# The first batch's start on one Trainium2 core: order of the q and k loads, tails first, and other zero products

## The chip, the core and the metric

The kernel runs on one core of a Trainium2 chip. The metric is the time of one execution on the device in microseconds (us), as the median of several runs; lower is better. A core has a matrix engine (TensorE, "PE" in the profile, its weight loads "PEld"), a vector engine (VectorE, DVE), a scalar engine (ScalarE, ACT), GpSimd (POOL) and a sync engine (SyncE, SP) that mostly issues transfers. Each engine works through its own list of instructions in order. Transfers run on 16 DMA engines; SP's go through one queue, GpSimd's through another.

## The reference, cut to what matters

Eight batches; 8 heads; 576 positions; head width 64; model width 512, hidden width 2048. First a linear attention whose features are scaled rectified values:

```python
def phi(x, c, s):
    r = np.maximum(x, 0.0)
    return np.concatenate([r * c, r * s], axis=-1)     # 64 -> 128 features
q_p, k_p = phi(q, cos_w, sin_w), phi(k, cos_w, sin_w)  # weights depend on the position alone
kv  = np.einsum('bhsf,bhsd->bhfd', k_p, v)
z   = np.sum(k_p, axis=2)
num = np.einsum('bhsf,bhfd->bhsd', q_p, kv)
den = np.einsum('bhsf,bhf->bhs', q_p, z)[..., None] + 1e-06
x   = num / den                                        # heads side by side: 576 x 512
```

Then a mixer: `h = x^T U V` (rank 32, over positions), `u = x + h^T`, and `out = u + relu(u w_ch1) w_ch2`.

## The kernel before

**Tiling.** The 576 positions of a batch are 64 groups of nine. An even partition of a 128-row tile holds a group's first five positions, an odd one its last four. So a batch's q is a tile `qst` of 128 partitions x 8 heads x 5 columns ("chunks") x 64: chunks 0 to 3 are full, chunk 4, the tail, has data in even partitions only. `load_even` fills all five chunks of the even partitions, `load_odd` four of the odd ones; k (`kst`) and v (`vst`) are laid out alike, and for batch 0 the tail chunk is set to zero first (lines 125 to 127), so that its odd rows are zero.

**Order.** The program is written out by hand: each engine's list follows the order of the Python statements (a manual schedule). Waits between engines come from semaphores at the true dependencies. From batch 1 on, a list of slots interleaves work; this case is about what lies ahead of it, batch 0.

**Batch 0.** `q_prep` (L305 on ScalarE, L307 on VectorE) makes one chunk's cosine or sine half from `qst`. `qtr_mm` (L394) transposes a chunk on TensorE, eight heads into one PSUM bank, and `qtr_evac` copies it to `q_pT` (tail: `q_tlT`). `k_prep` makes k's features; `z_mm` (L1219) sums them per head with a matrix of ones, in the order of `KORD`, into the bank `xz`, and `z_sb` is z in bf16. Then `first_chain`: `v0` is v in bf16, cast in four pieces of two heads; `kv0_mm` (L353) makes kv of heads 0 to 3, `den_mm` (L1227) the denominators of all heads, `recip` their reciprocals; `kv_unit(b, 1)` (L341) makes kv of heads 4 to 7; `xh_mm` (L1235) multiplies by kv, and `xh_norm` (L1244, VectorE) or `xh_norm_act` (L1267, ScalarE, chunk 3 of heads 0 to 3) divides. `a_mm` (L465), `open_mm` (L1258) and `uTd_mm` (L565) make u transposed; `g1_open` (L727) and `g1_main` (L710) are w_ch1's products, for which ScalarE makes `hid`. `g2_part` (L781) is w_ch2's product, from slot 16 on.

**Zero products.** `keep_warm` (L202) multiplies zeros by zeros, 512 columns wide or narrower, so that TensorE is busy before the data come; its results are not read.

**Gates.** `G_.tensor_copy(out=mark..., in_=X)` makes GpSimd wait for X before it issues the weight loads behind it (`w1_load`, `w2_load`, four each, one per quarter of the hidden width); a one-element transfer `nc.sync.dma_start(out=mark2, in_=X)` does the same on SP for the loads of batch 1.

Of the kernel before, what the change touches and what calls it, by code (L numbers as in the profile page):

```python
# [17 lines left out]
def kernel(  # L18
# [11 lines left out]
    nc = tc.nc  # L30

    B = 8
    H = 8
    S = 576
    D = 64
    E = D + 1
    P = 128
# [11 lines left out]
    def tail(b):  # L49
# [16 lines left out]
    qst, kst, vst = (  # L66
        pool.tile([P, H, 5, D], FP32, tag=n, bufs=1, name=n) for n in ("qst", "kst", "vst")
    )
# [4 lines left out]
    def load_even(dst, src, b, h0=0, h1=H):  # L73
        nc.sync.dma_start(
            out=dst[0:P:2, h0:h1].rearrange("m h c d -> m h (c d)"),
            in_=nines(src, b)[:, h0:h1, 0 : 5 * D],
        )

    def load_odd(dst, src, b, h0=0, h1=H):
        nc.sync.dma_start(  # L80
            out=dst[1:P:2, h0:h1, 0:4].rearrange("m h c d -> m h (c d)"),
            in_=nines(src, b)[:, h0:h1, 5 * D : 9 * D],
        )
# [19 lines left out]
            out=w1_bf[:, :, cs], in_=moe_w_ch1.rearrange("(d p) n -> p d n", p=P)[:, :, cs]  # L103
        )

    def w2_load(n):
        js = slice(n * 4, n * 4 + 4)
        nc.gpsimd.dma_start(
            out=w2_bf[:, js, :], in_=moe_w_ch2.rearrange("(j p) n -> p j n", p=P)[:, js, :]
        )  # L110

    def cast(eng, o, i):
        if eng is nc.scalar:
            nc.scalar.activation(out=o, in_=i, func=AF.Copy, bias=0.0, scale=1.0)  # L114
        else:
            eng.tensor_copy(out=o, in_=i)  # L116
# [5 lines left out]
    stU = st_uv[:, S : S + 5 * R].rearrange("p (c r) -> p c r", r=R)  # L122

    zero = pool.tile([P, 512], BF16, tag="o_sb", bufs=2, name="zero")
    V_.memset(zero, 0.0)
    for x in (qst, kst, vst):
        V_.memset(x[:, :, 4, :], 0.0)
    load_odd(qst, q, 0)
    load_even(qst, q, 0)
    load_odd(kst, k, 0)  # L130
    load_even(kst, k, 0)
    for h0 in (0, 4):
        load_odd(vst, v, 0, h0, h0 + 4)
        load_even(vst, v, 0, h0, h0 + 4)
# [264 lines left out]
    def qtr_evac(b, c, eng, t):  # L399
        if c < 4:  # L400
            cast(eng, q_pT[b][:, c, :, :], t)
        else:
            cast(eng, q_tlT[:, :, tail(b)], t[:, :, 0:P:2])
# [803 lines left out]


    TL = (0, 1, 2, 3, 4)
    KORD = (0, 1, 2, 4, 3)  # L1210

    z_sb = const.tile([P, H], BF16)

# [3 lines left out]
    def z_mm(b, c, z):  # L1217
        for h in range(H):
            nc.tensor.matmul(  # L1219
                out=z[:, h, :], lhsT=k_p[b][:, c, h, :] if c < 4 else k_tl[:, h, :],  # L1220
                rhs=ones, start=(c == 0 and h == 0), stop=(c == 3 and h == H - 1),
            )

    def den_mm(b, d, cs):
        for c in cs:
            for h in range(H):
                nc.tensor.matmul(  # L1227
                    out=d[:, c, h, :], lhsT=qT_of(b, c, h),
                    rhs=z_sb[:, h : h + 1].to_broadcast([P, 12]), start=True, stop=True,
                )  # L1230
# [32 lines left out]
    def xh_norm_act(b, c, h0, rec, acc):  # L1263
        x_alloc(b)
        rows = slice(0, P) if c < 4 else tail(b)
        for i in range(4):
# [3 lines left out]
                scale=rec[rows, c, h0 + i : h0 + i + 1],  # L1270
            )

    def first_chain(b, xz, z, v_ps):
        def fill(n):
            for _ in range(n):
                nc.tensor.matmul(
                    out=xz[:, 1, P:512], lhsT=zero[:, 0:P], rhs=zero[:, 0:384],
                    start=True, stop=True,
                )

        d = xz[:, 1, 0:480].rearrange("p (c h n) -> p c h n", h=H, n=12)
        rec = pool.tile([P, 5, H], FP32, tag="rec5", bufs=1, name="rec5")
        cast(V_, v0[:, 0:2], vst[:, 0:2])
        cast(V_, z_sb, z[:, :, 0])
        cast(V_, v0[:, 2:4], vst[:, 2:4])
        cast(V_, v0[:, 4:6], vst[:, 4:6])
        qtr_evac(b, 4, A_, t_q[4])
        kv_sb[b] = pool.tile([P, H, E], BF16, tag="kv", bufs=2, name="kv")
        acc = bank([P, 4, D], FP32, *G3, "kv_ps")
        kv0_mm(b, acc, (0, 1))  # L1290
        den_mm(b, d, (0, 1, 2))
        kv0_mm(b, acc, (2, 3))
        cast(A_, V_bf, v_ps.rearrange("r (c p) -> r c p", c=4))
        cast(A_, kv_sb[b][:, 0:4, 0:D], acc)
        cast(A_, v0[:, 6:H], vst[:, 6:H])
        den_mm(b, d, (3, 4))
        recip(rec, d[:, :, :, 0])
        x0 = [xh_mm(b, c, 0, *G3) for c in ORD[0:2]]
        kv_unit(b, 1, *T1, A_)
        x0 += [xh_mm(b, c, 0, *t) for c, t in zip(ORD[2:5], (G3, OA, OB))]  # L1300
        xh_norm_act(b, ORD[4], 0, rec, x0[4])
        for n in range(4):
            xh_norm(b, ORD[n], 0, rec, x0[n])
        x1 = [xh_mm(b, c, 4, *t) for c, t in zip(ORD[0:4], (G3, G3, G3, T1))]
        for n in range(2):
            xh_norm(b, ORD[n], 4, rec, x1[n])
        uT_alloc(b)
        a_ps = xz[:, 1, 0:P]
        a_mm(b, a_ps, (0, 1), range(5))
        cast(A_, A_of(b)[0:TS, :], a_ps[0:TS, :])  # L1310
        for i, (tag, bufs) in enumerate((OA, OB, T1)):
            uT_ps[b, i] = bank([P, 4, P], FP32, tag, bufs, "uT_ps")
        for i in range(2):
            open_mm(b, i, uT_ps[b, i], range(4))
        x1.append(xh_mm(b, ORD[4], 4, *G3))
        for n in range(2, 5):
            xh_norm(b, ORD[n], 4, rec, x1[n])
        for i in range(2):
            uTd_mm(b, i)
        for i in range(2):  # L1320
            uTd_evac(b, i, A_)
        a2 = bank([P, P], FP32, *G3, "a_ps")
        a_mm(b, a2, (2, 3), range(5))
        cast(V_, A_of(b)[TS:P, :], a2[TS:P, :])
        open_mm(b, 2, uT_ps[b, 2], range(4))
        u3 = ps.tile([P, 2, 512], FP32, tag="X", bufs=1, name="u3")
        uT_ps[b, 3] = u3[:, 0, :].rearrange("p (c t) -> p c t", c=4)
        open_mm(b, 3, uT_ps[b, 3], range(4))
# [1 line left out]
    FEATS = [(V_, V_ if c == 3 else A_) for c in TL]  # L1330
    qT_alloc(0)
    cast_uv()
    keep_warm(4, "X", 1)
    keep_warm(72, "X", 1, P)
    t_q = []
    for c in TL:
        tg = G3 if c < 3 else O2()
        t_q.append(bank([P, H, P], BF16, *tg, "t_ps"))
    for c in TL:
        q_prep(0, c, FEATS[c])  # L1340
        qtr_mm(0, c, 0, H, t_q[c])
        keep_warm(1, "X", 1)
    for c, eng in zip(TL[0:3], (V_, A_, V_)):
        qtr_evac(0, c, eng, t_q[c])
    xz = ps.tile([P, 2, 512], FP32, tag="X", bufs=1, name="xz")
    z = xz[:, 0, 0:384].rearrange("p (h n) -> p h n", n=48)
    v_ps = None
    for n, c in enumerate(KORD):
        k_prep(0, c, (V_, A_ if c < 4 else V_))
        if n < 2:  # L1350
            keep_warm((1, 2)[n], *T1)
        if n == 2:
            v_ps = spread_v(*T1)
        z_mm(0, c, z)
    qtr_evac(0, 3, A_, t_q[3])

    G_.tensor_copy(out=mark[0:1], in_=q_tl[0:1, 0, 0:1])
    w1_load(0)
    nc.sync.dma_start(out=mark2, in_=k_p[0][0:1, 0, 0, 0:1])
    load_odd(qst, q, 1)  # L1360
    load_even(qst, q, 1)
    first_chain(0, xz, z, v_ps)
    G_.tensor_copy(out=mark[0:1], in_=q_tlT[0:1, 0, 0:1])
    for n in range(1, 4):
        w1_load(n)
    nc.sync.dma_start(out=mark2, in_=z_sb[0:1, 0:1])
    load_odd(kst, k, 1)
    load_even(kst, k, 1)
    for h0 in (0, 4):
# [13 lines left out]

    def w2_all():
        G_.tensor_copy(out=mark[0:1], in_=q_pT[1][0:1, 3, 0, 0:1])
        for n in range(4):
            w2_load(n)

    at(6, w2_all)
# [109 lines left out]
```

## Time and profile before

| | us |
|---|---|
| median of 3 runs | 290.45 (290.09 to 290.92) |
| the profiled execution | 290.06 |
| its span, from first to last instruction | 288.3 |
| first product (of zeros) on TensorE | 1.19 |
| first features of q | 7.53 |
| first features of k | 11.16 |
| z in bf16 (`z_sb`) | 14.53 |
| first product with w_ch1 | 21.30 |
| first product with w_ch2 | 38.46 |

Times in a view are microseconds from the span's start. A row of the timeline gives the start, the length (of all its instructions together, where there are several), the engine, the line of the source, the operation, what it writes and from what, the shapes, the count, and in brackets how long the engine sat idle before and what ended that. An engine with the suffix q is its sequencer, which issues transfers. The granted clock was 1.00 throughout.

### The profile page before, as it was taken

What the parts mean: (1) busy time and instruction counts of PE and PEld (TensorE: products, weight loads), DVE (VectorE), ACT (ScalarE), POOL (GpSimd) and SP (SyncE); (2) the same over time, 40 slices, a digit from 0 to 9 for tenths busy, and PEclk for the clock granted to TensorE, in tenths of its full rate; (3) what the DMA queues carried; (4) which work ended last, traced back from release to release, by engine and by line L of the source; (5) the groups of instructions that cost most, each with busy time, mean ns of one, the idle gap of its engine ahead of it and who ended that gap; (6) DMA issues with size and microseconds to landing.
All of it is one profiled execution on the core that took longest, in us unless ns stands there. A gap on an engine that the chain in (4) does not pass through costs nothing.

```text
span 288.3 us, 7567 instructions
## 1 busy us (share of the span) xinstructions
PE 282.3 (98%) x3097; PEld 211.8 (73%) x3122; DVE 218.6 (76%) x449; ACT 179.7 (62%) x316; POOL 71.3 (25%) x111
## 2 busy tenths in 40 slices
PE   8999999999999999999999999999999999999995
PEld 6886455545887756876887667876888778899884
DVE  4979738886887688569895388958894689689864
ACT  2965651576687576986587588876797772177110
POOL 8330600050035304641006500351005000400140
PEclk9999999999999999999999999999999999999999
DMA  6999999999969999799829993489939400610023
GB/s 202 336 282 253 292 207 264 275 184 200 285 174 169 241 354 202 193 268 282 230 41 188 303 279 106 84 146 200 312 40 177 164 1 10 154 77 2 0 90 131
DMA packets 85447, 53.32 MB, mean 185 GB/s; under 512 B 53990, under 2 KB 83078, under 8 KB 85414
## 3 DMA queue, kind: packets, MB, share of 16 engines
q1 hardware_dynamic: 78998, 41.62, 61.5%
q0 software_dynamic: 6272, 11.17, 16.5%
q8 instruction: 24, 0.39, 0.5%
q10 hardware_dynamic: 144, 0.07, 0.1%
q14 instruction: 9, 0.07, 0.1%
HBM read 36.86 MB, written 9.44 MB: 161 GB/s over the span
## 4 chain that ended last, share of the span: by engine, by line
PE 97%; DVE 1%; issue 1%; DVEq 0%
PE w_ps L892 30%; PE g_ps L710 22%; PE al_ps L653 8%; PE be_ps L653 6%; PE gt_ps L741 5%; PE o_ps L781 5%; PE w_ps L202 3%; PE x_ps L439 3%; PE kv_ps L364 3%; PE ot_ps L801 2%; PE ot_ps L994 2%; PE a_ps L465 1%; PE va_ps L495 1%; PE t_ps L382 1%; PE t_ps L394 1%
## 5 line engine op out<-in xcount | busy, mean ns | idle before, releaser
L710 PE MATMUL g_ps<-uT,w_bf 128*128 128x512 bf16 x281 | 71.5, 380 | 0.7
L717 ACT ACTIVATE hid<-g_ps 128x512 bf16<-128x512 f32 x76 | 45.0, 597 | 26.2 <-PE g_ps L710 24.0
L912 POOL TENSOR_TENSOR o_sb<-o_sb,u_bf 128x512 f32<-128x512 f32 x21 | 25.6, 1232 | 110.6 <-DVE o_sb L912 110.6
L892 PEld LDWEIGHTS <-hid 128*128 128x128 bf16 x448 | 43.1, 98 | 5.7 <-DVE hid L857 0.2
L710 PEld LDWEIGHTS <-w_bf 128*128 128x128 bf16 x298 | 27.5, 98 | 23.8
L678 DVE TENSOR_TENSOR hid<-pw,be_ps 128x512 bf16<-128x512 f32 x39 | 26.7, 686 | 16.6 <-PE be_ps L653 9.4
L892 PEld LDWEIGHTS <-S 128*128 128x128 bf16 x336 | 32.2, 98 | 4.5
L114 ACT ACTIVATE pw<-al_ps 128x512 f32<-128x512 f32 x39 | 23.1, 595 | 15.4 <-PE al_ps L653 9.7
L892 PE MATMUL w_ps<-T,hid 128*128 128x256 bf16 x224 | 27.9, 273 | 0.0
L892 PE MATMUL w_ps<-w_bf,hid 128*128 128x256 bf16 x224 | 27.6, 273 | 0.0
L892 PE MATMUL w_ps<-T,S 128*128 128x256 bf16 x224 | 27.1, 273 | 0.0
L114 ACT ACTIVATE o_sb<-w_ps 128x512 f32<-128x512 f32 x21 | 12.5, 597 | 20.5 <-PE w_ps L892 14.1
L912 DVE TENSOR_TENSOR o_sb<-o_sb,w_ps 128x512 f32<-128x512 f32 x21 | 14.4, 685 | 13.7 <-ACT o_sb L114 9.6
L653 PEld LDWEIGHTS <-sa 128*128 128x128 bf16 x208 | 19.3, 98 | 4.9 <-issue 0.3
L506 DVE TENSOR_TENSOR u_bf<-x_bf,va_ps 128x1024 bf16<-128x1024 bf16 (+1 forms) x20 | 19.5, 1000 | 3.0 <-PE va_ps L495 3.0
L449 DVE TENSOR_TENSOR x_bf<-x_ps,rec 128x512 bf16<-128x512 f32 x28 | 19.4, 692 | 1.0
L116 POOL CAST v_ext<-vst 128x512 bf16<-128x512 f32 x24 | 16.4, 722 | 7.8 <-DMA vst<-in_v_dram 4.5
L653 PEld LDWEIGHTS <-w_bf 128*128 128x128 bf16 x156 | 15.2, 98 | 4.0 <-issue 0.2
L305 ACT ACTIVATE k_p<-kst,sinw 128x512 bf16<-128x512 f32 x26 | 18.0, 713 | 0.0
L741 PE MATMUL gt_ps<-uT_tl,w_bf 128*128 128x128 bf16 x256 | 16.4, 219 | 0.0
L653 PE MATMUL al_ps<-tb,sa 128*128 128x256 bf16 x104 | 15.6, 273 | 0.2
L781 PE MATMUL o_ps<-w_bf,hid 128*128 128x512 bf16 x61 | 15.3, 380 | 0.2
(192 smaller groups left out, 509.1 us busy)
## 6 DMA issues: line engine op xcount, KB each, us to landing
qst<-in_q_dram SPq DMA_DIRECT2D x14, 512.0 KB, 5.9
kst<-in_k_dram SPq DMA_DIRECT2D x14, 512.0 KB, 8.6
vst<-in_v_dram SPq DMA_DIRECT2D x12, 512.0 KB, 8.7
out_dram<-o_sb POOLq DMA_DIRECT2D x12, 512.0 KB, 6.7
w_bf<-in_moe_w_ch_dram POOLq DMA_DIRECT2D x8, 512.0 KB, 10.4
out_dram<-o_sb SPq DMA_DIRECT2D x4, 512.0 KB, 3.0
qst<-in_q_dram SPq DMA_DIRECT2D x2, 640.0 KB, 5.7
kst<-in_k_dram SPq DMA_DIRECT2D x2, 640.0 KB, 13.8
```

Source lines behind the costliest of these rows:

```text
L114: nc.scalar.activation(out=o, in_=i, func=AF.Copy, bias=0.0, scale=1.0)
L305: nc.scalar.activation(out=o, in_=i, func=AF.Relu, bias=0.0, scale=w)
L449: nc.vector.tensor_tensor(out=x_of(b, c, rows).rearrange("p (g i d) -> p g i d", g=2, d=D), in0=view[:, :, :, 0:D], in1=rec[rows].unsqueez ...
L506: nc.vector.tensor_tensor(out=u_bf[b][:, d0 : d0 + n], in0=x_bf[b].rearrange("p c (d n) -> p d c n", n=P)[:, d0 : d0 + n], in1=t.rearrange ...
L653: nc.tensor.matmul(out=res[:, k_, :], lhsT=lhs[:, d, k_, :], rhs=rhs[:, d, :], start=(opens and k_ == 0 and d == 0), stop=(k_ == 1 and d = ...
L678: V_.tensor_tensor(out=o, in0=x, in1=res, op=ALU.add)
L710: nc.tensor.matmul(out=g_ps.rearrange("p (c t) -> p c t", c=4), lhsT=w1_bf[:, d, j * P : j * P + P], rhs=uT[b][:, d, :, :], start=(d == 0) ...
L717: nc.scalar.activation(out=hid[b][:, j, :], in_=g_ps, func=AF.Relu, bias=0.0, scale=1.0)
L741: nc.tensor.matmul(out=g_ps[:, jj, :], lhsT=w1_bf[:, d, j * P : j * P + P], rhs=uT_tl[pr][:, d, :], start=(d == 0), stop=(d == 3),)
L781: nc.tensor.matmul(out=o, lhsT=hid[0][:, j, cc * P : cc * P + P], rhs=w2_bf[:, j, :], start=(j == 0), stop=(j == NJ - 1),)
L892: nc.tensor.matmul(out=res[:, g, :], lhsT=lhs[:, k_, g * P : g * P + P], rhs=rhs[:, k_, :], start=(opens and k_ == 0 and g == 0), stop=(k_ ...
L912: eng.tensor_tensor(out=o_, in0=x, in1=y, op=ALU.add)
```

## The change

- `qst`'s tail chunk is set to zero before the tile `zero`, not after it.
- q's odd rows are loaded in two halves of four heads; the order is odd heads 0 to 3, all even rows, odd heads 4 to 7. For k the even rows come first.
- q's features are made in the order tail, 0, 1, 2, 3, and k's likewise; k's tail takes its sine from ScalarE and chunk 3 from VectorE, where it was the other way round. `z_mm` starts with the tail.
- Ahead of the features there are 13 zero products of 512 columns for 4 of 512 and 72 of 128; between the transposes the counts are 2, 1, 1, 0, 1 for one each; 18 wide ones in all ahead of z. The three of `keep_warm` between the k chunks go, and four of 384 columns (`fill`, which was there unused) take their place.
- Evictions and casts are dealt anew. The tail's transposed tile goes from ScalarE to VectorE, between q's features; chunk 2 from VectorE to ScalarE, after k's features; chunk 3 from ScalarE to VectorE, in `first_chain`. `v0` of heads 4 and 5 goes to ScalarE and of heads 6 and 7 to VectorE. `V_bf` is cast ahead of the first chain; `spread_v` comes between q's transposes.
- Denominators are made in the order 4, 0, 1 and 2, 3.
- The gates of w_ch1's loads and of batch 1's k and v wait for other tiles.
- w_ch2's first quarter is loaded in two transfers.

```diff
-    def w2_load(n):
-        js = slice(n * 4, n * 4 + 4)
+    def w2_load(n, i=0, w=4):
+        js = slice(n * 4 + i, n * 4 + i + w)
...
+    V_.memset(qst[:, :, 4, :], 0.0)
     V_.memset(zero, 0.0)
-    for x in (qst, kst, vst):
+    for x in (kst, vst):
         V_.memset(x[:, :, 4, :], 0.0)
-    load_odd(qst, q, 0)
+    load_odd(qst, q, 0, 0, 4)
     load_even(qst, q, 0)
+    load_odd(qst, q, 0, 4, H)
+    load_even(kst, k, 0)
     load_odd(kst, k, 0)
-    load_even(kst, k, 0)
...
-    KORD = (0, 1, 2, 4, 3)
+    KORD = (4, 0, 1, 2, 3)
...
-                rhs=ones, start=(c == 0 and h == 0), stop=(c == 3 and h == H - 1),
+                rhs=ones, start=(c == KORD[0] and h == 0), stop=(c == KORD[-1] and h == H - 1),
...
         cast(V_, v0[:, 2:4], vst[:, 2:4])
-        cast(V_, v0[:, 4:6], vst[:, 4:6])
-        qtr_evac(b, 4, A_, t_q[4])
+        qtr_evac(b, 3, V_, t_q[3])
...
         kv0_mm(b, acc, (0, 1))
-        den_mm(b, d, (0, 1, 2))
+        den_mm(b, d, (4, 0, 1))
         kv0_mm(b, acc, (2, 3))
-        cast(A_, V_bf, v_ps.rearrange("r (c p) -> r c p", c=4))
         cast(A_, kv_sb[b][:, 0:4, 0:D], acc)
-        cast(A_, v0[:, 6:H], vst[:, 6:H])
-        den_mm(b, d, (3, 4))
+        cast(A_, v0[:, 4:6], vst[:, 4:6])
+        cast(V_, v0[:, 6:H], vst[:, 6:H])
+        den_mm(b, d, (2, 3))
...
-    keep_warm(4, "X", 1)
-    keep_warm(72, "X", 1, P)
+    keep_warm(13, "X", 1)
...
-    for c in TL:
+    v_ps = None
+    for n, c in enumerate(ORD):          # ORD = (4, 0, 1, 2, 3)
         q_prep(0, c, FEATS[c])
         qtr_mm(0, c, 0, H, t_q[c])
-        keep_warm(1, "X", 1)
-    for c, eng in zip(TL[0:3], (V_, A_, V_)):
+        if n == 2:
+            qtr_evac(0, 4, V_, t_q[4])
+        if n == 3:
+            v_ps = spread_v(*T1)
+        else:
+            keep_warm((2, 1, 1, 0, 1)[n], "X", 1)
+    k_prep(0, 4, (V_, A_))
+    for c, eng in ((0, V_), (1, A_)):
         qtr_evac(0, c, eng, t_q[c])
...
-    v_ps = None
-    for n, c in enumerate(KORD):
-        k_prep(0, c, (V_, A_ if c < 4 else V_))
-        if n < 2:
-            keep_warm((1, 2)[n], *T1)
-        if n == 2:
-            v_ps = spread_v(*T1)
+    z_mm(0, 4, z)
+    for c in KORD[1:]:
+        fill(xz, 1)
+        k_prep(0, c, (V_, A_ if c < 3 else V_))
         z_mm(0, c, z)
-    qtr_evac(0, 3, A_, t_q[3])
-
-    G_.tensor_copy(out=mark[0:1], in_=q_tl[0:1, 0, 0:1])
+    cast(A_, V_bf, v_ps.rearrange("r (c p) -> r c p", c=4))
+    qtr_evac(0, 2, A_, t_q[2])
+
+    G_.tensor_copy(out=mark[0:1], in_=q_p[0][0:1, 3, 0, D : D + 1])
     w1_load(0)
...
-    G_.tensor_copy(out=mark[0:1], in_=q_tlT[0:1, 0, 0:1])
+    G_.tensor_copy(out=mark[0:1], in_=q_pT[0][0:1, 2, 0, 0:1])
     for n in range(1, 4):
         w1_load(n)
-    nc.sync.dma_start(out=mark2, in_=z_sb[0:1, 0:1])
+    nc.sync.dma_start(out=mark2, in_=q_pT[0][0:1, 3, 0, 0:1])
...
-        for n in range(4):
+        for i in (0, 2):
+            w2_load(0, i, 2)
+        for n in range(1, 4):
             w2_load(n)
```

More of the change, by code (lines that the diff above doesn't have):

```diff
@@ L1271, in xh_norm_act, with fill @@
             )
-    def first_chain(b, xz, z, v_ps):
[L1274 to L1279, printed above, removed]
+    def fill(xz, n):
+        for _ in range(n):
+            nc.tensor.matmul(
+                out=xz[:, 1, P:512], lhsT=zero[:, 0:P], rhs=zero[:, 0:384],
+                start=True, stop=True,
+            )
+    def first_chain(b, xz, z, v_ps):
         d = xz[:, 1, 0:480].rearrange("p (c h n) -> p c h n", h=H, n=12)
```

## The prediction, made before the changed kernel ran

> **What bounds the kernel now.** I read the page's busy table first, then busy time by stage, then the opening of the timeline, and last the chain of waits for the zero products. Page, parts 1 and 4:
>
> ```profile
> PE 282.3 (98%) x3097; PEld 211.8 (73%) x3122; DVE 218.6 (76%) x449; ACT 179.7 (62%) x316; POOL 71.3 (25%) x111
> PE 97%; DVE 1%; issue 1%; DVEq 0%
> ```
>
> TensorE looks full from end to end, but at the start it is filled with products of zeros, so the share says nothing there. Busy time by stage (PE, PEld, DVE, ACT, POOL; then granted clock, DMA share, GB/s):
>
> ```profile
> 0.00:10.00 10.00, 8.76 (x93) 7.32 (x94) 5.58 (x19) 4.15 (x7) 8.14 (x29) 1.00 0.79 244
> 10.00:21.00 11.00, 10.84 (x235) 8.81 (x233) 9.14 (x25) 8.97 (x19) 3.46 (x6) 1.00 1.15 304
> 21.00:38.00 17.00, 16.84 (x119) 8.66 (x122) 13.56 (x26) 11.23 (x22) 4.43 (x9) 1.00 1.17 262
> 61.00:288.00 227.00, 223.06 (x2437) 174.86 (x2452) 174.38 (x348) 145.36 (x253) 51.67 (x62) 1.00 0.70 164
> ```
>
> From about 21.3, where w1's first product starts, TensorE does real work with 1 to 2% idle. So the change is worth what it moves that moment, as long as no later load then comes too late. Ahead of it the Scalar and Vector engines carry a chain (timeline: start, length, engine, line, out<-in, count, idle before and releaser):
>
> ```profile
> 7.53 1.95 ACT L305 ACTIVATE q_p<-qst,sinw 128x512 bf16<-128x512 f32 x3 [2.52 <-DMA qst<-in_q_dram]
> 9.39 0.71 ACT L305 ACTIVATE q_tl<-qst,sinw 128x512 bf16<-128x512 f32 x1
> 10.24 1.02 ACT L114 ACTIVATE q_pT<-t_ps 128x1024 bf16<-128x1024 bf16 x1
> 11.16 2.55 ACT L305 ACTIVATE k_p<-kst,sinw 128x512 bf16<-128x512 f32 x4
> 13.48 0.48 DVE L307 TENSOR_SCALAR k_p<-kst,cosw 128x512 bf16<-128x512 f32 x1
> 14.53 0.17 DVE L116 CAST z_sb<-xz 128x8 bf16<-128x8 f32 x1 [0.16 <-PE xz L1219]
> 15.84 0.39 ACT L114 ACTIVATE kv<-kv_ps 128x256 bf16<-128x256 f32 x1 [0.25 <-PE kv_ps L353]
> 16.12 0.73 ACT L114 ACTIVATE v<-vst 128x640 bf16<-128x640 f32 x1
> 17.39 0.39 ACT L114 ACTIVATE kv<-kv_ps 128x256 bf16<-128x256 f32 x1 [0.54 <-PE kv_ps L341]
> 17.76 0.93 ACT L1267 ACTIVATE x_bf<-xh_ps,rec 128x64 bf16<-128x64 f32 x4
> ```
>
> Both engines idle until q has landed at 7.5; from then on neither rests until z is summed. k's last bytes land at 11.06 by the trace's landing records, just as the k features begin (11.16).
>
> **The loads.** The same bytes of q and k go through one queue that is already full (about 350 GB/s from 6 to 12 us), so q should be complete at 7.5 and k at 11.1 as before. What moves is the order. q's even rows, the only ones with the tail column, are followed by 256 KB more instead of by nothing. 256 KB take some 0.75 us at that rate, so q's tail can start at about 6.75. k's even rows come ahead of 512 KB, 1.5 us: k's tail is there at about 9.6. The cosine and sine tables are ready (the last one at 5.0). SP issues one load more, 0.65 us; its loads are issued by 7 and data flow until 14, so nothing. Memset of qst ahead of zero: the even load waits on it less, and the first product starts 0.48 later (one memset row), at 1.67.
>
> **Vector engine, q to z.** Features cost 0.40 each back to back (k rows at 12.69, 13.09, 13.48), 0.43 for the first q ones; an eviction of 1024 columns 0.65 (10.06 to 10.90 with a wait, 0.68 long); the tail's transposed tile, evicted on ScalarE before, took 0.69 on VectorE in batch 1. Before: six q features, two evictions, six k features, 7.55 to 13.96. After: the q tail's cosine goes ahead into idle time, then two q features (7.55 to 8.38), tail eviction (9.0), three q features (10.2), k's tail cosine (10.6), one eviction (11.25), four cosines and one sine of k, done at 13.3. The tail eviction is a new wait on TensorE's tail transposes, with three q features behind it; the tail's sine is done at 7.5, eight transposes take 0.6, so it is clear at 8.2 against 8.4. Gain 0.65.
>
> **ScalarE.** Tail sine at 6.8; three q sines 7.53 to 9.39; k's tail sine to 10.0; eviction to 11.05; then three k sines instead of four plus an eviction and a tail eviction: 11.13 to 13.07. V_bf 0.60 and q_pT chunk 2 at 1.02 follow, to 14.5, ahead of the denominators that need it (14.7).
>
> **TensorE.** The zero products ended at 9.09 before, 0.8 behind the first features. Now 13 wide ones, started 0.43 apart while cold (weight loads of the first ones at 1.59, 2.02, 2.45), end at 7.1 to 7.3 and free the queue. z's last chunk starts at 13.5 for 14.13, z_sb at 13.9 for 14.53. Denominators follow 0.22 later (14.1), the second pair of kv heads 0.58 after that (14.7), ScalarE's kv cast 0.51 after that: 15.2 for 15.84. Gain still 0.65. The four short fills lie in waits for features: nothing; the cover gone, 0.16 each.
>
> **The redeal takes some back.** Before, ScalarE's v cast at 16.12 fed heads 6 and 7 alone, and heads 4 and 5 ran at 16.52 beside it. Now it holds heads 4 and 5: it runs 15.5 to 16.2, all four heads wait behind it (20 products, start at 16.25, 0.125 a head, 0.25 to drain), and the second kv cast starts at 17.0 for 17.39. The four normalizations behind it on ScalarE, then A, uT and w1's first product keep that 0.4. VectorE's side (reciprocal at 15.7 for 16.57, with v0's last cast and q_pT chunk 3 in between) gains 0.8 and waits. **Sum: 0.65 - 0.25 = 0.4.**
>
> **Behind it.** The first w2 product is due at 38.46 and w2's first quarter lands at 37.9 (issued 30.20, 7.7 to landing):
>
> ```profile
> 30.20 2.97 POOL L108 DMA_DIRECT2D w_bf<-in_moe_w_ch_dram  x4 [0.28 <-issue]
> 38.46 1.03 PE L781 MATMUL o_ps<-w_bf,hid 128*128 128x512 bf16 x4
> ```
>
> With 0.4 off it is due at 38.06, 0.15 after landing; in two halves the first is there some 2.5 us sooner (512 KB took 5.0 us behind w1's last load, landed at 32.9), and the second is due two products, 0.43, later. So the split covers gains up to 0.9. Its price is a fifth issue, 0.74, on GpSimd: V_qt's copies behind it move from 33.1 to 33.9, first used after 60. The three w1 quarters wait for q_pT chunk 2 on ScalarE (14.5) instead of the tail's eviction (15.1); w1's first quarter for the last q feature (10.2, as before); batch 1's k for q_pT chunk 3 (15.0, where SP got there at 16.5). w1's quarters land 1.4 us or more ahead of use. Nothing.
>
> The profiled execution took 290.06 (span 288.3 and 1.8 around it), 0.4 below the median of 290.45; I take 0.4 off both: 289.65, and **290.1** as the median to come (290.05 rounded). Bounds: DVE's and ACT's part add some 25 rows at 0.02 of doubt, half a microsecond: -0.1 to 0.9 of gain.
>
> **Rivals.**
> *Cold TensorE* (slower). The chain of waits, first asked whole and then from 7 us:
>
> ```profile
> 3.13 5.96 PE w_ps L202 x72
> 6.92 2.18 PE w_ps L202 x38
> ```
>
> The last 38 take 0.057 each, the 34 ahead of them 3.79 us, 0.11 each: TensorE doubled its rate at about 6.9, 5.7 us after its first product, though the granted clock stands at 1.00 throughout. Thirteen products fill only 5.6 us from 1.67. If the rate then stays low, the queue from 7.55 holds 40 transposes (0.107) and 6 wide products (0.43), 6.9 us: z cannot come before 14.4, and ScalarE's eviction of chunk 1 waits to 11.4 and pushes k's sines by 1.3. That is 0.9 to 1.7 later than my sum, 0.5 to 1.3 slower than before: **291.4**. It decides if the rate rises after about 10.5. Against it: the same clock time of 6.9 would still be covered, and the gap is short.
> [...]
>
> *The whole gain arrives* (faster). If ScalarE's v cast starts earlier than 15.5 or VectorE's side sets the end, 0.8 comes through, and a little more from wide products no longer in TensorE's way before z: 0.8 to 1.2, **289.45**. For it: VectorE is the fuller of the two at 17 to 19 us. Against: four normalizations on ScalarE stand behind the late cast.
>
> *Nothing* (no change). VectorE's list has no slack from 7.55 to 15.4; a tail eviction that waits 0.4, or k whose last rows land that much later, eats it all: **290.45**.
>
> **Chances.** My sum 0.45, the whole gain 0.27, nothing 0.12, cold 0.16. A measurement of this kernel tells about 0.3%, 0.87 us, from no change. Three quarters of the whole gain and a fifth of my sum's spread lie over that: faster 0.3. Cold, and a little from a VectorE list that overruns, lies over it on the other side: slower 0.2. The same: 0.5. My sum's own range is 289.6 to 290.5; with the other cases 289.2 to 291.2.
>
> **What would show it.** Right: tail features on both engines before 7.5; k features from 11.1 with no tail among them; z_sb near 13.9; ScalarE's second kv cast near 17.0; w1's first product near 20.9; no stall at the first w2 product. Wrong: 128-wide transposes over 0.1 apart after 7.5 (cold); a gap on VectorE ahead of the tail eviction; k features after 11.4; x normalizations, not the ScalarE cast, ahead of A; or a stall near 38.

## The result, and the profile after

The changed kernel takes 292.64 us (median of 10 runs, 291.07 to 300.6), the kernel before 290.29 on the same chip (10 runs, 289.91 to 291.62). The ratio is 1.0069, 95% interval 1.0046 to 1.0092: some 2 us slower, where 290.1 and no more than 291.2 had been forecast. Runs more than 1.5% above the fastest of their kernel are left out of ratios here and of ratios, medians and ranges below; here it is the one at 300.6, whose mean granted clock was 0.977, and without it the median is 292.46, 2.2 above before. The profiled execution took 291.94, span 290.2, granted clock 1.00.

Page, parts 1 and 4, of the changed kernel:

```profile
PE 281.1 (97%) x3036; PEld 206.9 (71%) x3060; DVE 219.9 (76%) x450; ACT 179.5 (62%) x315; POOL 70.1 (24%) x112
PE 86%; DMA 8%; DVE 2%; issue 1%; ACT 0%; POOL 0%; SPq 0%; DVEq 0%; POOLq 0%
```

TensorE was 97% of the chain that ended last and is 86% now; 8% are DMA. Busy time by stage (PE, PEld, DVE, ACT, POOL; clock, DMA share, GB/s):

```profile
0.00:10.00 10.00, 7.33 (x36) 3.10 (x37) 5.48 (x18) 4.27 (x8) 8.04 (x29) 1.00 0.79 242
10.00:21.00 11.00, 10.12 (x221) 7.84 (x218) 10.19 (x27) 7.76 (x17) 3.65 (x6) 1.00 1.09 283
21.00:38.00 17.00, 16.84 (x128) 8.86 (x128) 12.95 (x25) 11.35 (x22) 5.22 (x10) 1.00 1.17 260
```

VectorE did 10.19 us of work between 10 and 21 where it did 9.14: its list is denser, but it is not earlier. The opening of the timeline:

```profile
1.73 5.45 PE L204 MATMUL w_ps<-zero 128*128 128x512 bf16 x13 [1.73 <-DVE zero L126]
7.25 0.72 ACT L307 ACTIVATE q_tl<-qst,sinw 128x512 bf16<-128x512 f32 x1 [2.23 <-DMA qst<-in_q_dram]
8.13 1.95 ACT L307 ACTIVATE q_p<-qst,sinw 128x512 bf16<-128x512 f32 x3 [0.16 <-DMA qst<-in_q_dram]
9.99 0.71 ACT L307 ACTIVATE k_tl<-kst,sinw 128x512 bf16<-128x512 f32 x1
11.51 1.94 ACT L307 ACTIVATE k_p<-kst,sinw 128x512 bf16<-128x512 f32 x3
13.72 0.47 DVE L309 TENSOR_SCALAR k_p<-kst,sinw 128x512 bf16<-128x512 f32 x1
14.66 0.17 DVE L116 CAST z_sb<-xz 128x8 bf16<-128x8 f32 x1
16.03 0.39 ACT L114 ACTIVATE kv<-kv_ps 128x256 bf16<-128x256 f32 x1 [1.19 <-PE kv_ps L355]
17.87 0.39 ACT L114 ACTIVATE kv<-kv_ps 128x256 bf16<-128x256 f32 x1 [0.83 <-PE kv_ps L343]
18.24 0.93 ACT L1269 ACTIVATE x_bf<-xh_ps,rec 128x64 bf16<-128x64 f32 x4
```

The first sine of a full chunk of q starts at 8.13 for 7.53, z_sb is cast at 14.66 for 14.53, and the second kv cast starts 0.48 later. What TensorE waits for from 6 us on (engine, line, releaser: total, times, longest):

```profile
PE t_ps L396 <- ACT q_tl L307: 0.8, 1, 0.8
PE x_ps L441 <- DMA q_pT<-q_p: 0.8, 1, 0.8
PE kv_ps L343 <- ACT v L114: 0.2, 1, 0.2
PE xz L467 <- issue: 0.2, 1, 0.2
...
PE o_ps L783 <- DMA w_bf<-in_moe_w_ch_dram: 0.2, 1, 0.2
```

From 6 to 285 us the kernel before has no wait in this view. The second line is new and far from the change: at 199 us, the DMA that transposes batch 6's q. The last one is w2's:

```profile
30.81 2.92 POOL L108 DMA_DIRECT2D w_bf<-in_moe_w_ch_dram  x4 [0.28 <-issue]
39.08 0.59 PE L783 MATMUL o_ps<-w_bf,hid 128*128 128x512 bf16 x2
39.84 0.59 PE L783 MATMUL o_ps<-w_bf,hid 128*128 128x512 bf16 x2 [0.17 <-DMA w_bf<-in_moe_w_ch_dram]
```

Three more executions of the changed kernel were traced (f4, g2, g3 below). Against the kernel before (span 288.28, w1's first product at 21.30, w2's at 38.46), all in us:

| execution | time | span | q's first full sine | z_sb | w1's first product | w2's second half late by | wait at q_pT | sum of the three losses | longer span |
|---|---|---|---|---|---|---|---|---|---|
| profiled | 291.94 | 290.16 | 8.13 | 14.66 | +0.61 | 0.34 | 0.83 | 1.78 | 1.88 |
| f4 | 291.22 | 289.37 | 7.76 | 14.29 | +0.11 | 0 | 0.88 | 0.99 | 1.09 |
| g2 | 293.49 | 291.73 | 8.40 | 14.58 | +0.40 | 0 | 2.95 | 3.35 | 3.45 |
| g3 | 291.29 | 289.52 | 8.51 | 14.79 | +0.74 | 0 | 0.40 | 1.14 | 1.24 |

So these four are accounted for to 0.1 us: on average 0.47 from the opening, 0.09 from w2, and 1.27 from the transposing DMA, which is issued at 189 to 190 us and needed near 198. (The profile shows 0.17 of w2's 0.34 as idle time; 0.34 is the delay from one product's start to the next.) All four ran at full clock. Of the ten timed runs five were below 0.998; the four of them in the comparison (0.994, the figure of e4's traced execution, whose one stretch of 3.41 us at half rate is worth 1.7 us) took 292.46 to 295.0, the five others 291.07 to 292.83, with a median of 291.44. So about half of the loss of 2.2 us is there in runs at full clock, and the rest comes with the runs at 0.994, of which none was traced.

### The profile page after: what moved, and what is told of

It reads as the page before. It is cut to its first block, busy times and chain, and to the rows that moved or that the text cites. A ratio compares the mean times of both kernels' runs of the same rounds, so it can differ in the third digit from the quotient of the medians.

```text
span 290.2 us, 7442 instructions
## 1 busy us (share of the span) xinstructions
PE 281.1 (97%) x3036; PEld 206.9 (71%) x3060; DVE 219.9 (76%) x450; ACT 179.5 (62%) x315; POOL 70.1 (24%) x112
## 4 chain that ended last, share of the span: by engine, by line
PE 86%; DMA 8%; DVE 2%; issue 1%; ACT 0%; POOL 0%; SPq 0%; DVEq 0%; POOLq 0%
PE w_ps L894 30%; PE g_ps L712 18%; PE al_ps L655 7%; PE be_ps L655 5%; PE gt_ps L743 5%; PE o_ps L783 5%; DMA q_pT<-q_p 3%; PE x_ps L441 3%; DMA w_bf<-in_moe_w_ch_dram 3%; PE ot_ps L803 2%; PE ot_ps L996 2%; PE kv_ps L366 2%; DMA qst<-in_q_dram 2%; PE a_ps L467 1%; PE va_ps L497 1%
## 5 line engine op out<-in xcount | busy, mean ns | idle before, releaser
L307 ACT ACTIVATE k_p<-kst,sinw 128x512 bf16<-128x512 f32 x25 | 17.3, 712 | 0.0
L116 POOL CAST v_ext<-vst 128x512 bf16<-128x512 f32 x24 | 14.4, 641 | 7.4 <-DMA vst<-in_v_dram 4.1
```

The source lines that it names most:

```text
L307: nc.scalar.activation(out=o, in_=i, func=AF.Relu, bias=0.0, scale=w)
```

## Experiments

The kernel before was timed beside each group of runs; its median was 290.26 to 290.44 throughout, and none of these runs was below 0.998. "Clock" counts runs below 0.998, out of all runs.

**One part undone or done alone.**

e1, the changed kernel with more zero products:
```diff
-    keep_warm(13, "X", 1)
+    keep_warm(17, "X", 1)
```


> The changed kernel with 17 wide zero products ahead of the first features in place of 13 (0.22 us each once TensorE is fast, so they end at about 8.0, where the tail's features are ready, in place of 7.2). The clock theory: in about half of the ten timed runs of the changed kernel the mean granted clock was 0.994, which is one stretch of 3.4 us at half rate, and those runs are 2 us longer (median 293.5 for 291.4 of the runs at 1.000); too few zero products cause it, so here the clock is 1.000 in all or nearly all runs and the median is 291.3 to 291.5. The loads theory: q complete 0.6 us late is a loss of its own, so the runs at clock 1.000 stay at 291.1 to 291.9, about 1.1 over before. If neither: the share of 0.994 runs is as large as in the changed kernel and the median stays near 292.6.

e2, the changed kernel with before's load order:
```diff
-    load_odd(qst, q, 0, 0, 4)
+    load_odd(qst, q, 0)
     load_even(qst, q, 0)
-    load_odd(qst, q, 0, 4, H)
-    load_even(kst, k, 0)
     load_odd(kst, k, 0)
+    load_even(kst, k, 0)
```


> The changed kernel with the loads of before: all of q's odd rows, then its even rows, k's odd rows, k's even rows, four transfers for five. The loads theory: the split order spreads the finish of a transfer over the 16 DMA engines (landing records: q's even rows 5.6 to 7.2, last odd ones 6.9 to 8.0; before 7.0 to 7.4), so q's first full features move back from 8.13 to about 7.55, w1's first product from 21.9 to 21.3 or earlier, the second half of w2's first quarter lands before it is due, and runs at clock 1.000 come to 289.9 to 290.4. The clock theory: the zero products still end at 7.2 with nothing until 8.2, so some runs show a clock of 0.994 and 2 us more. The redeal theory (the new order of features, casts and evictions loses by itself): q at 7.55 but z_sb no earlier than 14.5 and runs at 1.000 still at 291.

e3, e2 and before's zero products as well:
```diff
-    keep_warm(13, "X", 1)
+    keep_warm(4, "X", 1)
+    keep_warm(72, "X", 1, P)
```


> The changed kernel with the loads of before and the zero products of before (4 wide and 72 narrow ones ahead of the features): what is left is the order tail first, the casts and evictions dealt anew, the gates, and w2's first quarter in two. Loads and clock theories together: no run below a clock of 1.000, median 290.0 to 290.5 (the 0.4 us forecast for the redeal less the 0.5 that the zero products, ending at 9.1, hold up the tail's transposes). Redeal theory: above 290.9.

e4, the kernel before with the new zero products alone:
```diff
-    keep_warm(4, "X", 1)
-    keep_warm(72, "X", 1, P)
+    keep_warm(13, "X", 1)
```


> The kernel before with 13 wide zero products in place of 4 wide and 72 narrow ones, nothing else. TensorE is then free from about 6.9 until q's first features at 8.3, for a chunk's transposes 0.6 earlier than before. Clock theory: several of the runs show 0.994 or lower and 2 us more, median over 291. Loads theory alone: every run at 1.000 and the median 290.0 to 290.4.

| run | median (range) | ratio to before | clock |
|---|---|---|---|
| e1 | 290.56 (289.98 to 292.92) | 1.0020 [1.0000, 1.0040] | 0 of 12 |
| e2 | 292.27 (291.91 to 293.14) | 1.0070 [1.0049, 1.0090] | 0 of 6 |
| e3 | 291.68 (291.15 to 292.88) | 1.0047 [1.0027, 1.0066] | 0 of 8 |
| e4 | 292.84 (291.18 to 294.62) | 1.0078 [1.0042, 1.0115] | 7 of 10 |

Four more zero products give back 1.9 us of the 2.2, and 13 of them alone cost the kernel before 2.6 us. The zero products are the costly part. (e1's traced execution was its second longest, 292.60. It lost 0.30 by w1's first product, 1.0 in two delays near 39.6 and 42.3, and 0.97 at the transposing DMA, so the places of the loss are still there with 17 products. A run of e1 near its median was not traced.)

e2 takes as long as the changed kernel, and e3, whose zero products are before's, 1.4 us more than before. In e2 q's last load lands between 7.00 and 7.37, as in the kernel before, but nothing comes of it: before's order brings k's even rows last, and the new order of work wants the tail's features, which need them, first (k_tl's sine at 11.02 in e2 for 9.99, z_sb at 15.31 for 14.66); order of loads and order of work belong together. e2 also has the 13 wide products, and none of its six runs lost the clock, against what the clock theory expected.

The trace of e4 shows one way in which the zero products cost time. Up to 18 us it is as the kernel before (z_sb 14.53, second kv cast 17.39, both the same); then (its waits, and its busy time by stage):

```profile
PE xz L465 <- issue: 1.8, 1, 1.8
```
```profile
17.07:20.48 3.41, 1.51 (x41) 1.23 (x39) 2.63 (x8) 1.30 (x5) 1.21 (x2) 1.00 1.14 315
20.48:23.89 3.41, 3.41 (x38) 2.49 (x39) 0.72 (x2) 1.23 (x3) 0.00 (x0) 0.50 1.18 239
```

TensorE stands for 1.8 us with nothing to wait for ("issue"), and its clock is halved for the next 3.41 us. The DMA queue table has a queue of the kind "instruction" that carries nothing but packets of 16384 bytes (the line is the changed kernel's: packets, MB, share of the engines). The changed kernel's trace has 6120 TensorE instructions, 255 for each of the 24.

```profile
q8 instruction: 24, 0.39, 0.6%
```

The trace records when each packet starts. The first one starts at 13.43 in the kernel before and 17.91 in e4. A zero product is two TensorE instructions, weight load and product: 4 + 72 of them are 152 instructions, 13 are 26. With 126 fewer ahead of it, TensorE gets through its instructions later (to the 256th recorded one at 15.00 in e4, at 12.51 in the kernel before), and the first packet starts 2.9 us behind that one in e4, 0.9 in the kernel before. In e4 batch 1's q, issued at 12.89 and landed at 20.08, is then on the DMA engines. (That the packets feed TensorE, that their time follows its progress, and that this one comes late because of q, is inferred.)

That TensorE stands for want of instructions is inferred too, from all nine traces that have such a stall ("issue", 0.2 to 1.9 us): it falls behind 449 or 450 recorded TensorE instructions in every one of them, whichever product is next (`a_mm` in five, `xh_mm` in four), and it ends 2.2 to 2.6 us after the start of the first packet, which itself starts anywhere from 16.66 to 18.59.

**Cover or supply.** Theory A is this reading, the instruction supply: with fewer instructions ahead of q the first packet comes later and TensorE stands (17.91 and 1.8 us in e4, 13.43 and 0 before). Shorter zero products could also cost because they leave TensorE idle sooner and it loses its clock: that is theory B, an assumption here. So the same cover with more instructions, and more cover with few.

e5 and e6, the kernel before with 54 narrow or 23 wide ones:
```diff
-    keep_warm(4, "X", 1)
-    keep_warm(72, "X", 1, P)
+    keep_warm(54, "X", 1, P)     # e5;  e6: keep_warm(23, "X", 1)
```


> The kernel before with 54 narrow zero products (128 columns) for 4 wide and 72 narrow ones. Cover: about 0.11 each while slow, to about 7.5 us, as long as the 13 wide ones last; instructions: 108 with their weight loads, against 26. [...] Theory B (too little cover: TensorE idles between 7.5 and 10 and the clock is taken back for it): runs at 0.994 and below as with 13 wide ones, median above 292.

> The kernel before with 23 wide zero products (512 columns) for 4 wide and 72 narrow ones. Cover: to about 9 us as before; instructions: 46 against 152. Theory A (instruction supply): the first 16384-byte packet no earlier than 16.5, a stall of TensorE of up to 1.8 us near 18.7 and some runs at 0.994 or below, median above 291. Theory B (cover): no such runs, 290.3 +- 0.6, since the zero products last as long as before.

e7, the changed kernel with 54 narrow ones, and e8, the same with q's odd rows in one load:
```diff
-    keep_warm(13, "X", 1)
+    keep_warm(54, "X", 1, P)     # e7, e8
-    load_odd(qst, q, 0, 0, 4)
+    load_odd(qst, q, 0)          # e8
     load_even(qst, q, 0)
-    load_odd(qst, q, 0, 4, H)    # e8
```


> The changed kernel with 54 narrow zero products for 13 wide ones. Theory A (instruction supply): first packet of the instruction queue at about 14.5 for 16.66, no run at 0.994, and the median falls from 292.6 to about 290.5 to 291.4 (the changed kernel's runs at full clock had 291.1 to 291.9; the 0.6 us by which q's features start later and what hangs on it stay). Theory B (cover): as the changed kernel, 292 to 293 with some runs at 0.994.

> As the run before (changed kernel with 54 narrow zero products), and q's odd rows in one load ahead of its even rows instead of two halves around them; k's even rows stay ahead of its odd ones. Theory C (the split order makes q complete 0.6 us later): the first sines of q's full chunks at 7.5 to 7.6 for 8.15, though the tail's come no earlier than 7.45, z_sb 0.3 to 0.6 earlier than in the run before, and the time 0.3 to 0.8 us lower. Theory D (q is complete when its bytes have passed, whatever the order; the later start is from something else, such as k's even rows, which follow): first full sines at 8.1 again, the time as the run before or up to 0.5 higher for the later tail.

f1, the kernel before with 28 wide ones, since e6's had ended at 7.95 and not at 9.1:
```diff
-    keep_warm(4, "X", 1)
-    keep_warm(72, "X", 1, P)
+    keep_warm(28, "X", 1)
```


> The kernel before with 28 wide zero products for 4 wide and 72 narrow ones: they last to about 9.0 us, as before (23 wide ones ended at 7.95), with 56 instructions against 152. Theory A (instruction supply): the first packet of the instruction queue after 16.5 us as with 23 wide ones, a stall of TensorE of 0.5 to 1.8 us put down to issue between 18 and 20.5, median 290.9 to 291.5, some runs at 0.994. Theory B (cover alone): no stall that matters, all runs at 0.998 or more, 290.3 +- 0.4.

| run | zero instructions | first packet | stall on issue, traced | median (range) | ratio | clock |
|---|---|---|---|---|---|---|
| before | 152 | 13.43 | 0 | | | 0 |
| e5 | 108 | 13.44 | 0 | 291.47 (290.19 to 293.05) | 1.0031 [1.0009, 1.0053] | 4 of 12 |
| e6 | 46 | 17.00 | 0.9 | 291.31 (290.44 to 293.81) | 1.0035 [1.0012, 1.0057] | 3 of 12 |
| f1 | 56 | 18.59 | 1.9 | 291.93 (290.81 to 294.35) | 1.0053 [1.0030, 1.0076] | 5 of 12 |
| e7 | 108 | 13.70 | 0 | 290.73 (290.00 to 293.93) | 1.0015 [0.9992, 1.0039] | 1 of 12 |
| e8 | 108 | 13.65 | 0 | 291.03 (290.45 to 291.88) | 1.0016 [1.0000, 1.0032] | 0 of 12 |

f1 is the plainest: its zero products last longer than before's, to 9.75, TensorE has no gap ahead of q's transposes, and yet (its waits, then busy time by stage):

```profile
PE xh_ps L1235 <- issue: 1.9, 1, 1.9
```
```profile
16.21:19.62 3.41, 2.47 (x73) 2.15 (x69) 2.13 (x7) 2.77 (x9) 2.41 (x4) 1.00 1.06 330
19.62:23.03 3.41, 2.24 (x46) 1.76 (x48) 1.83 (x5) 0.48 (x2) 0.00 (x0) 1.00 1.14 224
```

That is theory A, and cover alone cannot explain it. e7 agrees: no more cover than 13 wide products (its zero products ended at 6.36), four times the instructions, 1.7 us less than the changed kernel. Over all traces the stall grows with the time of the first packet: none at 13.4 to 16.6, 0.2 at 16.66 and 16.85, 0.3 at 17.41, 0.9 at 17.00, 1.8 at 17.91 and 18.06, 1.9 at 18.59 (f2 and f3, below, with 0.6 at 16.66 and 0.8 at 17.01, show a scatter of about half a microsecond). e5 is half a miss: its first packet is early and its trace has no stall, but its median is above the 290.3 +- 0.6 that theory A gave it, and four of its runs were below 0.998. Its zero products end at 7.11 for 9.09, so too little cover may cost the clock as well; e7 and e2, versions of the changed kernel with no more cover (6.36 and 7.14), speak against it (1 of 12 and 0 of 6). For e1 the two cannot be told apart: its four products are more cover and only eight more instructions.

e8 was meant for the loads. q's even rows landed at 7.03 to 7.56 over the 16 DMA engines, so theory C is right on the landing; but the tail's sine then goes first (timeline of e8):

```profile
7.64 0.72 ACT L306 ACTIVATE q_tl<-qst,sinw 128x512 bf16<-128x512 f32 x1 [2.63 <-DMA qst<-in_q_dram]
8.27 1.32 ACT L306 ACTIVATE q_p<-qst,sinw 128x512 bf16<-128x512 f32 x2
```

The full chunks start at 8.27, z_sb is at 14.69, and the 0.3 to 0.8 us that theory C expected over e7 are not there.

**What the other parts are worth.** Both on e1's 17 zero products.

f2, two gates on earlier work:
```diff
-    G_.tensor_copy(out=mark[0:1], in_=q_p[0][0:1, 3, 0, D : D + 1])
+    G_.tensor_copy(out=mark[0:1], in_=q_p[0][0:1, 2, 0, D : D + 1])
     w1_load(0)
-    nc.sync.dma_start(out=mark2, in_=k_p[0][0:1, 0, 0, 0:1])
+    nc.sync.dma_start(out=mark2, in_=k_tl[0:1, 0, 0:1])
```


> The changed kernel with 17 wide zero products, and two gates moved to earlier work: w1's first quarter waits for q's chunk 2 instead of 3, batch 1's q for k's tail features instead of k's first full chunk. Theory E (the stream behind is late because these two gates open 0.6 to 0.9 later than before): w1's first quarter is issued near 10.4 for 11.3, batch 1's q near 12.5 for 13.2, w1's quarters land 0.6 to 1.5 earlier, the second half of w2's first quarter no longer makes TensorE wait at 39.6 (0.2 us), and the time is 0.2 to 0.6 below the run with 17 zero products (290.56). Rival: w1's first quarter shares the queue with k and v, k lands later, z_sb 0.2 to 0.5 later than 14.35, and the time is the same or up to 0.5 higher.

f3, w2's first quarter in one load:
```diff
-        for i in (0, 2):
-            w2_load(0, i, 2)
-        for n in range(1, 4):
+        for n in range(4):
             w2_load(n)
```


> The changed kernel with 17 wide zero products, and w2's first quarter in one load again. If the split covers what the prediction says: the first w2 product waits for the whole quarter, which lands at about 39.5 (second half with the split), so TensorE waits 0.6 to 0.9 at 38.8 and the time is 0.4 to 0.9 above the run with 17 zero products (290.56). If the split does nothing: 290.56 +- 0.3.

f2: 291.09 (290.63 to 292.05), 1.0026 [1.0013, 1.0039]; no better than e1, so theory E's 0.2 to 0.6 are missed. Its trace had z_sb at 14.17 and no wait for w2, and then a stall on issue of 0.6 us. f3: 290.89 (290.12 to 293.38), 1.0015 [0.9995, 1.0035]; the expected 0.4 to 0.9 did not show in the time, and its trace can't tell, since a stall of 0.8 us had moved the first w2 product to 39.51 and nothing waited for w2.

**The changed kernel traced again.** f4, g2 and g3 are the changed kernel as it is, g4 is e4 again, and g1 is the changed kernel with 68 narrow zero products, which last to 7.7.
```diff
-    keep_warm(13, "X", 1)
+    keep_warm(68, "X", 1, P)     # g1
```


> The changed kernel once more, for a second trace. About half of its runs have a granted clock of 0.994, one window of 3.4 us at half rate. If this execution is one of them: by theory A (late instructions) TensorE stalls on issue by 1 us or more between 18 and 20.5, and the half-rate window begins at the end of the window that holds the stall; by theory B (cover) the half-rate window begins between 8 and 11, behind the gap that follows the zero products. At clock 1.00: the stall on issue is 0.3 or less, as in the first trace.

> The changed kernel with 68 narrow zero products for 13 wide ones: they last to about 8.0 us (no gap before the tail's transposes) and are 136 instructions. Theory A (instruction supply is what the 13 wide ones cost; the loads and the redeal cost little): the first instruction packet near 13.5, no stall on issue, no run below 0.998, 290.0 to 290.6. Rival (the uneven landing of q, 0.6 us, stays on the path): 290.7 to 291.2, as with 54 narrow ones.

> The changed kernel, for a trace at 0.994. Theory A: then a stall on issue of 1 us or more near 18 to 20.5, in a window of 3.4 us that is busy for less than half, and half rate in the next window. Theory B: the window with the gap behind the zero products (7 to 10) is the one with less than half, and half rate begins near 10. At clock 1.00: first packet of instructions near 16.5, stall at most 0.3, 291.2 to 291.9.

> As the look before: the changed kernel, for a trace at 0.994. Theory A: a stall on issue of 1 us or more near 18 to 20.5 ahead of the half-rate window; theory B: half rate from near 10 on.

> The kernel before with 13 wide zero products once more. Its first trace had a stall on issue of 1.8 us at 18.7 and half rate from 20.48 to 23.89. Theory A: a stall of 1 us or more again, the first packet of instructions after 17; half rate after it if one window holds most of it. Theory B: the stall is absent in some executions and the half rate, if any, begins near 10.

g4 repeated e4: first packet at 18.06, 1.8 us on issue, half rate from 20.68 to 24.09. None of f4, g2, g3 ran at 0.994; the question they were for stays open. They gave the table above instead, and g2 the longest wait of all (its waits, then busy time by stage):

```profile
PE x_ps L441 <- DMA q_pT<-q_p: 3.0, 1, 3.0
PE t_ps L396 <- ACT q_tl L307: 2.0, 1, 2.0
```
```profile
4.74:8.15 3.41, 1.44 (x7) 0.47 (x5) 0.58 (x1) 0.99 (x3) 2.52 (x8) 1.00 1.05 341
8.15:11.56 3.41, 3.35 (x41) 2.40 (x42) 3.14 (x8) 3.16 (x6) 2.07 (x7) 1.00 1.09 353
```

Here the zero products had run out at 6.2, TensorE stood for 2.0 us, and the clock was kept. So the gap that theory B named did not cost it, in this run, in g3, where it was 2.7, and in e7's trace, where it was 3.0.

g1: 290.81 (290.17 to 291.91), 1.0016 [1.0000, 1.0032], clock 0 of 12, first packet at 13.57, no stall. The packet, the stall and the clock are as theory A said; the time is in the range of the rival (290.7 to 291.2), and still not below before. It is the price of the loads, the redeal and the w2 split with about as many zero products as before: between nothing and 0.3%. Its profiled execution took 290.17, the shortest of the twelve, with w1's first product at 21.48 (+0.18).

**The transposing DMA issued at 190 us.** In the four traces of the changed kernel the DMA's first half landed 9.91, 9.98, 12.04 and 9.50 us after its issue, and TensorE needs it some 9.1 after; in the kernel before it took 8.43, in g1 7.65. In the same four an instruction packet starts 0.66 to 1.00 us after that issue; in the kernel before the packets lie 5.9 ahead and 10.1 behind, in g1 5.6 and 10.7. The change took 124 instructions out of TensorE's program (6120 in the trace for 6244), and every later packet falls elsewhere. So the packet was moved, by padding TensorE's program near 57 us with one-column products that nobody reads (28 on the changed kernel, 76 on g1):
```diff
+    def pad(n):
+        w_ps = ps.tile([P, 512], FP32, tag="X", bufs=1, name="w_ps")
+        for _ in range(n):
+            nc.tensor.matmul(out=w_ps[:, 0:1], lhsT=ident, rhs=ident[:, 0:1], start=True, stop=True)
+    at(30, lambda: pad(28))      # h1;  h2: 76
```


> The changed kernel with 28 one-column products (56 instructions) added near 45 us, whose results nobody reads; they cost 1 to 3 us there, which the trace gives. They bring the later instruction packets some 2.5 us earlier against the work (256 instructions took 11.35 us there). Theory F (the packet among the transposing load's own packets makes batch 6's load slow): the packet near 190 now starts about 1.5 us ahead of the load's issue, the load's first half lands within 8.7 us of its issue (9.5 to 12.0 in the four traces of the changed kernel), and TensorE does not wait for it. Rival G (something else in the changed kernel makes it slow): first half at 9.5 or more, a wait of 0.4 us or more.

> The changed kernel with 68 narrow zero products, and 76 one-column products (152 instructions) added near 45 us, whose results nobody reads; they cost 4 to 7 us there. They bring the instruction packet that was 10.7 us behind the transposing load's issue to about 1 us behind it. Theory F: the load's first half lands 9.5 us or more after its issue (7.65 without the padding), and TensorE waits 0.4 us or more for it. Rival G: 7.5 to 8.7, no wait.

The first product that reads the transposed q (timelines, one line each), in g2 and h1, and then in g1 and h2:

```profile
201.09 0.43 PE L441 MATMUL x_ps<-kv,q_pT 128*128 128x65 bf16 x8 [2.95 <-DMA q_pT<-q_p]
```
```profile
199.75 0.42 PE L441 MATMUL x_ps<-kv,q_pT 128*128 128x65 bf16 x8
```
```profile
197.77 0.42 PE L441 MATMUL x_ps<-kv,q_pT 128*128 128x65 bf16 x8
```
```profile
202.05 0.43 PE L441 MATMUL x_ps<-kv,q_pT 128*128 128x65 bf16 x8 [0.42 <-DMA q_pT<-q_p]
```

In h1 the packet starts 1.46 ahead of the issue, the first half lands after 5.91, and no wait is left behind 60 us. In h2 it starts 1.19 behind, the first half lands after 9.51, and TensorE waits 0.42. Theory F held in both directions, in one trace each. All 20 traces side by side agree with it: in the ten that have a packet between 0.3 ahead of the issue and 1.8 behind it the first half landed after 8.5 to 12.0, in the ten others after 5.9 to 8.4 (these bounds are chosen with the traces in hand). It is not the whole condition for a wait: in e4 and g4 the packet is 0.99 and 0.96 behind and the first half landed after 8.6 and 8.5, in time; and with the packet 0.2 to 0.5 ahead it landed after 10.06 in e1's trace (a wait of 1.0), but after 8.53 and 8.31 in those of f2 and f3. The times can't show it: the paddings took 0.84 and 2.04 us of TensorE and 0.5 of waiting each (1 to 3 and 4 to 7 were expected), h1 took 293.44 (two of six runs below 0.998) and h2 294.62 (one of four).

## Why the prediction was wrong

**The loads: the step "q should be complete at 7.5 and k at 11.1 as before" failed.** In the kernel before q's last load landed between 6.96 and 7.43 over the 16 DMA engines. In the changed one the even rows landed between 5.61 and 7.17 and the second half of the odd rows between 6.93 and 8.05: hardly later on average (7.43 for 7.21), but a feature waits for the slowest engine. The full chunks started 0.23 to 0.98 later (7.76 to 8.51 for 7.53), where the term was 0. The tail came at 6.81 to 7.75, not 6.75, and k's last rows at 11.01 to 11.97.

**VectorE's gain of 0.65 was right in size.** From the first full chunk to z_sb it took 6.98 before, 6.16 to 6.51 in the four traces and 6.31 in g1: 0.47 to 0.82 less. The late start took it back: z_sb at 14.29 to 14.79 in the four traces, not 13.9.

**The redeal's 0.25 was right.** From the first kv cast to the second: 1.55 before, 1.84 after, a loss of 0.29. With nothing gained ahead of it, it became a loss: w1's first product 0.11 to 0.74 later, where it should have been 0.4 earlier.

**The zero products, booked as nothing, were the largest term.** The step ("end at 7.1 to 7.3 and free the queue") asked when they end and whether TensorE warms up under them. It did not ask how many instructions they are. 126 fewer ahead of q move the first instruction packet from 13.4 into batch 1's q (16.3 to 16.9 in the four traces, at the edge of a stall), and all later packets with it: in the changed kernel one falls on the transposing DMA at 190 us, worth 0.4 to 3.0. With four more wide products, or with 54 or 68 narrow ones, 1.7 to 1.9 us of the 2.2 are gone (e1, e7, g1).

**The cold rival did not happen.** It named 291.4, near three of the four traced times by luck, for a cause that no trace shows: in all four TensorE's rate rose under the zero products, at 4.47 (g3), 4.74 (g2), 6.30 (f4) and 6.77 (the profiled execution), from one per 427 ns to one per 216. The trace's record of the granted clock begins only there, which is why the views have 1.00 ahead of it too. The first product started at 1.73 in each, so the rise came after 2.74 to 5.04 us of products, where it had taken 5.7 in the kernel before; over the 20 traces of this study it came between 4.40 and 7.42. What sets the moment was not shown, and the rival's chance of 0.16 was the author's estimate.

**w2.** The first w2 product came at 38.57 to 39.20, later than the 38.06 it was due at, and still the second half was once not there: the stream had moved. w1's quarters landed at 25.94, 30.32 and 34.90 in the profiled execution for 24.11, 28.5 and 32.92, though they were issued 0.3 earlier. A load of batch 1's q that was issued 0.6 later is not the whole reason: in f2 it was issued 0.85 earlier than before, and the quarters still landed at 24.89, 29.38 and 33.73. w1's first quarter, forecast to be issued at 10.2 as before, was issued at 11.59 and landed at 17.41 for 17.58. The split covered the first half and left 0.17 of waiting on the second in one of the four. That it covers more was not shown (f3).

**What stays open.** Where the timed runs of the changed kernel at 0.994 lose their clock, and with it about half of the loss; e4 and g4 suggest the stall on issue, but in this kernel's four traces it was 0.25 at most. Why e5, h1 and h2 have such runs too, and e2, with 13 wide products, has none. Why w1's later quarters land 0.7 to 2.0 late. Why the same packet slows the transposing DMA past its due time in one kernel and not in another. No version beat the kernel before: e1, e7 and g1 lie 0.15 to 0.2% above it by their ratios, with intervals that reach down to no difference.

## What to carry to other kernels

When instructions are taken out of an engine's list, count them as well as their time: here 126 fewer moved the first instruction packet from 13.43 to 17.91 (e4), and with 124 fewer in the changed kernel a later one started 0.66 to 1.00 us behind the issue at 190 us, so look in the trace at what the packets will fall on. The load split in two for an earlier first part was as late as its slowest DMA engine (8.05, for a mean of 7.43); read the spread of the landings, not the bytes by the rate. And a wait that appears 180 us behind the edit can be the edit's, as the 0.4 to 3.0 us near 199 were.

## What the runs showed of the hardware

- The queue of the kind "instruction" carries 24 packets of 16384 bytes over the kernel, 0.88 to 1.56 us each in the changed kernel's trace, and TensorE stood for 1.9 us where the first of them started at 18.59 (f1) instead of 13.43. In the nine traces with such a stall it came behind 449 or 450 recorded instructions and ended 2.2 to 2.6 us after the packet's start. Nothing in the busy table shows it; the waits name it "issue".
- The transposing DMA of batch 6 was slower with such a packet near its issue: its first half took 8.5 to 12.0 us with one between 0.3 ahead and 1.8 behind, 5.9 to 8.4 otherwise (ten traces each, and one moved packet in each direction, h1 and h2).
- In e4 and g4 TensorE ran at half rate for one stretch of 3.41 us (20.48 to 23.89, 20.68 to 24.09). In the 3.41 us ahead of it TensorE was busy for 1.51 and 1.48, both with a stall of 1.8 in one piece. Stretches as long with 1.44 (g2) or 1.57 (g3, e7) busy, with zero products and a gap of 2.0 to 3.0, were not followed by half rate; nor were the two that f1's stall of 1.9 lay across (2.47 and 2.24 busy). The busy share of the profile alone does not tell.
- One DMA engine of the 16 was late by itself: in e7's trace 15 of q's last landings came by 8.12 and one at 9.27, and k's by 9.96 and one at 11.36.
